# Another order of the parts in a convolution's list of four steps, with the table loads where they stand

## The chip, the cores and the metric

The kernel runs on one core of a Trainium2 chip. The time is device time of one execution, in microseconds (us); the median of three runs counts. Times in rows of the profile are from the start of the span.

## The reference: what is computed

A block with two halves. The first modulates a layer norm of the 2048 x 640 input by two rows computed from a condition, convolves each of the 640 channels along the 2048 positions with a kernel that a state-space model gives, adds a skip term and a gated residual. The second is a gated MLP on the same pattern. Cut to the first half:

```
h = layernorm(x) * (1 + ca) + sa
P = exp(dt * A * l)                       # 640 channels x 128 states x 2048 positions, complex
K = einsum("dn,dnl,dn->dl", C, P, dt * B).real
y = irfft(rfft(pad(h)) * rfft(pad(K)))[:2048] + h * Dskip
x = x + ga * y
h = layernorm(x) * (1 + cb) + sb
x = x + gb * ((silu(h @ w1) * (h @ w3)) @ w2)
```

## The kernel before, in words

A position is split as 64 a + b. So the convolution's kernel K for a channel is a product of a slow table (32 entries) and a fast one (64), each 128 states wide, and the states are summed by TensorE. The work goes by steps k of 16 channels, 40 in all. The transforms are matmuls with fixed tables, in two stages each way; their steps run ten behind (LAG), because the spectrum of a group of 128 channels needs the kernels of eight steps.

Each step has parts, and each part runs on one engine:

- PH (L442, POOL): the phases of the 16 channels, integer products and an add. Its buffer is one of four, freed by A2 of four steps earlier.
- AB, CO, SI (L450 to L461, ACT): absolute value of the phases, then cosine and sine. CO and SI use ACT's sine table; AB and plain copies run under any table.
- PA, PQ (L398, L409, PE): the exponents of the fast and the slow table, as small matmuls into PSUM; inside the list both write the one bank with the tag "B". XA, XQ (L421, L426, ACT): their exponentials, read from that bank into the table A. They use ACT's exponential table. So PA(k), XA(k), PQ(k), XQ(k), PA(k+1) follow one another by necessity.
- E1, E2, A1, A2 (L469 to L483, DVE): table times cosine (E1, E2, into E) and times sine (A1, A2, in place), in two pieces each.
- kg (L489, PE): the sum over states, 64 small matmuls. K (L499, DVE): out of PSUM, with skip term and gate. pt (L508, PE): the first transform stage of the kernel. uk (L516, ACT): copies it to where the spectra stand.
- st (L533, PE): the second stage, for input and kernel together, into one PSUM tile (L544). It loads its table from HBM (256 KB, three buffers), and every second st also loads a part of the next channel group's input spectra (u_load, L523).
- kc (L550, ACT): copies the kernel's spectrum out of PSUM. T, Y (L556, L565, DVE): products and sums of the complex product, partly in the same PSUM tile, which the next st reuses.
- iv (L574, PE): the first inverse stage; it loads its table (256 KB, three buffers). zt (L591, ACT): every second step, copies its result out of PSUM and stores it in two pieces to HBM.

A step's parts in the list carry a number: "XA+4" in round r is XA of step 4 r + 4. The list (L789) holds four steps' worth of words, and the loop at L797 runs it ten times. A word whose step is out of range, or was done before, does nothing; with what the code ahead of the loop has done, the rounds with r = 2 to 8 compute exponentials of steps 12 to 39, and r = 9 has none left. E1 of steps 24, 26, 28 and 30 also issues the load of one input tile (L802).

Inside the loop every instruction of PE, DVE, POOL and ACT is held in program order (`keep`, L113, and `act`, L117), so the list is the order on these four engines. DMAs go on SP's queue; the tile framework's planner places them by its own due times, and they wait there one behind the other. ACT's table loads are in no list: they are put in wherever an exponential follows a sine or cosine, or the other way round. Behind the loop (L805) the remaining convolution steps, loads for the MLP and the first row statistics run; the MLP follows.

Of the kernel before, what the change touches and what calls it, by code (L numbers as in the profile page):

```python
# [92 lines left out]
def tile_kernel(ctx: ExitStack, tc: tile.TileContext, a):  # L93
# [53 lines left out]
    uk = kp.tile([P, 3, NA, DC], F32, name="uk")  # L147
# [589 lines left out]
    for tk in range(LAG):  # L737
# [49 lines left out]


    ROUND = (  # L789
# [5 lines left out]
    ).split()  # L795
    in_order[0] = True
    for rnd in range(NS // EB):  # L797
# [293 lines left out]
```

## Time and profile before

| | us |
|---|---|
| median of 3 runs | 1058.37 |
| lowest, highest | 1058.28, 1059.08 |
| the profiled execution's own time | 1055.13 |
| its span, from the first to the last instruction | 1053.0 |
| mean granted TensorE clock | 0.921 |

Busy over the span: PE 963.9 us (92%), DVE 617.0 (59%), ACT 515.1 (49%), POOL 254.1 (24%). The rounds with exponentials and their table loads lie from about 169 to 380 us, the rest of the convolution to about 450, the MLP from about 467 to the end.

How to read it: in a windows row, the first number is the window's length, then each engine's busy time with its count of instructions, then the granted TensorE clock (1.00 is full), the DMA engines' busy share and GB/s. In a timeline row, start and duration, then engine, line, operation and tiles; in brackets the idle time before it and what ended it. In the chain of waits, each row is a piece of the chain that ended last, followed back from the end. In a waits row: who waited for whom, the total, how often, the longest. The tile `A` holds the tables, `cs` and `ph` cosine and sine, `pa` and `pq` the exponents, `pk` the sums over states, `p` the spectra, `pz` the inverse's first stage, `s` and `i` the loaded tables.

### The profile page before, as it was taken

The numbers are of one execution on the slowest core, as the hardware profiler recorded it, in microseconds if no ns is written. First come the engines' busy times: TensorE is split into PE (matmuls) and PEld (weight loads), VectorE is DVE, ScalarE is ACT, GpSimd is POOL, SyncE is SP. The second block draws the span as 40 slices with busy tenths as digits, with TensorE's granted clock in tenths as the row PEclk, the third lists the DMA queues.
The fourth block names the chain that finished last, engine by engine and source line by source line (L and its number), as shares of the span: only waits on it lengthen the run. The fifth ranks groups of instructions, "written<-read, shape, count | busy, mean of one in ns | idle before, by whom it ended". The sixth has DMA issues, their size and how long they took to land.

```text
span 1053.0 us, 20326 instructions
## 1 busy us (share of the span) xinstructions
PE 963.9 (92%) x8324; PEld 716.2 (68%) x8324; DVE 617.0 (59%) x1024; ACT 515.1 (49%) x697; POOL 254.1 (24%) x213
## 2 busy tenths in 40 slices
PE   5897888889888898759999999999999999999997
PEld 2444454666666675437778877788877788888886
DVE  4698774888788876655543465444555543533332
ACT  3658574898788873233234433234432344333331
POOL 1633431444343412131111111211111211111110
PEclk9655686999899989969999999999999999999999
DMA  9463493354354458877543364443353233433311
GB/s 268 161 251 115 179 249 91 113 161 130 111 144 134 129 159 187 267 188 212 144 123 97 89 205 132 119 119 88 101 186 100 83 96 98 139 99 101 95 43 50
DMA packets 107040, 146.29 MB, mean 139 GB/s; under 512 B 20836, under 2 KB 62948, under 8 KB 106948
## 3 DMA queue, kind: packets, MB, share of 16 engines
q1 hardware_dynamic: 104500, 140.09, 45.2%
q0 software_dynamic: 1024, 2.49, 0.9%
q10 hardware_dynamic: 1424, 2.43, 0.8%
q8 instruction: 65, 1.06, 0.4%
q14 instruction: 27, 0.22, 0.1%
HBM read 118.76 MB, written 26.21 MB: 138 GB/s over the span
## 4 chain that ended last, share of the span: by engine, by line
PE 74%; ACT 14%; DVE 6%; DMA 3%; issue 3%; POOL 0%; SPq 0%; DVEq 0%; ACTq 0%; POOLq 0%
PE acc L952 17%; PE pg L938 6%; PE pg L939 6%; PE pg L940 6%; PE pu L940 6%; PE pu L939 6%; PE pu L938 6%; PE p L544 5%; ACT cs L119 3%; PE pa L406 3%; ACT A L119 3%; ACT ph L119 2%; PE pq L418 2%; ACT L119 2%; PE pt L513 2%
## 5 line engine op out<-in xcount | busy, mean ns | idle before, releaser
L971 POOL TENSOR_TENSOR w<-w,gbr 128x512 f32<-128x512 f32 x55 | 83.7, 1522 | 395.6 <-DMA w<-in_w_dram 372.5
L446 POOL TENSOR_TENSOR ph<-thi,iota 128x1024 int32<-128x1024 int32 x40 | 85.4, 2134 | 207.0 <-DVE A L482 136.3
L938 PE MATMUL pg<-xh,gh 128*128 128x512 f32 x280 | 112.0, 400 | 0.1
L939 PE MATMUL pg<-xl,gh 128*128 128x512 f32 x280 | 109.6, 391 | 1.1 <-DVE xl L911 1.1
L923 ACT CAST gh<-wg 128x640 fp32r<-128x640 f32 x55 | 40.2, 731 | 141.8 <-PE pg L939 141.8
L940 PE MATMUL pg<-xh,gl 128*128 128x512 f32 x280 | 109.4, 391 | 0.0
L924 DVE TENSOR_TENSOR gl<-wg,gh 128x640 fp32r<-128x640 f32 x55 | 51.3, 933 | 89.5 <-ACT gh L923 88.4
L939 PE MATMUL pu<-xl,uh 128*128 128x512 f32 x260 | 101.2, 389 | 0.0
L938 PE MATMUL pu<-xh,uh 128*128 128x512 f32 x260 | 101.2, 389 | 0.0
L940 PE MATMUL pu<-xh,ul 128*128 128x512 f32 x260 | 101.1, 389 | 0.0
L924 DVE TENSOR_TENSOR wl<-w,wh 128x640 fp32r<-128x640 f32 x55 | 47.9, 870 | 88.6 <-ACT wh L923 88.6
L987 DVE TENSOR_TENSOR hf<-pu,sg 128x512 f32<-128x512 f32 x52 | 36.0, 692 | 102.8 <-PE pu L940 101.8
L544 PE MATMUL p<-uk,s 128*64 128x256 f32 x640 | 89.8, 430 | 1.6 <-DMA s<-in_s_dram 1.6
L923 ACT CAST uh<-wu 128x640 fp32r<-128x640 f32 x51 | 37.3, 732 | 106.4 <-issue 67.4
L952 PE MATMUL acc<-wh,hh 128*128 128x512 f32 x224 | 87.6, 391 | 0.0
L952 PE MATMUL acc<-wl,hh 128*128 128x512 f32 x224 | 87.2, 389 | 0.0
L923 ACT CAST wh<-w 128x640 fp32r<-128x640 f32 x55 | 40.1, 729 | 91.6 <-PE acc L952 91.1
L952 PE MATMUL acc<-wh,hl 128*128 128x512 f32 x208 | 80.9, 389 | 0.0
L544 PEld LDWEIGHTS p<-uk,s 128*64 128x64 f32 x640 | 47.7, 154 | 36.1 <-issue 15.7
L938 PEld LDWEIGHTS pg<-xh,gh 128*128 128x128 f32 x280 | 52.6, 188 | 17.8 <-issue 5.6
L585 PE MATMUL pz<-Y,i 64*128 64x128 f32 x640 | 48.0, 291 | 14.9 <-ACT zt L122 6.9
L939 PEld LDWEIGHTS pg<-xl,gh 128*128 128x128 f32 x280 | 52.6, 188 | 13.1 <-DVE xl L911 2.9
(203 smaller groups left out, 2072.8 us busy)
## 6 DMA issues: line engine op xcount, KB each, us to landing
wg<-in_wg_dram SPq DMA_DIRECT2D x55, 320.0 KB
wu<-in_wu_dram SPq DMA_DIRECT2D x51, 320.0 KB
w<-in_w_dram SPq DMA_DIRECT2D x51, 320.0 KB
us<-u SPq DMA_DIRECT2D x16, 640.0 KB
s<-in_s_dram SPq DMA_DIRECT2D x40, 256.0 KB
i<-in_i_dram SPq DMA_DIRECT2D x40, 256.0 KB
uk<-us SPq DMA_DIRECT2D x32, 256.0 KB
zs<-zt SPq DMA_DIRECT2D x32, 256.0 KB
```

The lines of the kernel that those rows point to most:

```text
L119: return tc.keep_in_program_order(S.activation(*args, **kw))
L446: hold(G.tensor_tensor(p, bc(thi[:, sl], 2, NPH), bc(iota, 1, SD), op=OP.mult))
L544: keep(PE.matmul(p2[par * 64:par * 64 + 64, pi, c, :], s2[:, pi * 2 + par, c * 64:c * 64 + 64], uk[:, 0:kn + 1:kn, f, :], start=True, stop ...
L585: ins = keep(PE.matmul(pz[:, par, (g % 2) * 2 + pi, :], i1[r, pi, c, :], Y[r, pi, c, :], start=(c == 0), stop=(c == 1), tile_position=(par ...
L923: S.copy(hi, src)
L924: V.tensor_tensor(lo, src, hi.bitcast(F32), op=OP.subtract)
L938: PE.matmul(ps, wh, xh, start=(i == 0), stop=False)
L939: PE.matmul(ps, wh, xl, start=False, stop=False)
L940: PE.matmul(ps, wl, xh, start=False, stop=(i == n - 1))
L952: PE.matmul(acc[k], lhs, rhs, start=(f == 0 and i == 0), stop=(f == NFT - 1 and i == len(terms) - 1))
L971: G.tensor_tensor(w2r[:, :512], w2r[:, :512], gbr, op=OP.mult)
L987: V.tensor_tensor(hf, pu, sg, op=OP.mult)
```

## The change

The one list is replaced by another; nothing else is touched. Both hold a word for every part of four steps. Some words carry another number, which moves them past the end of a round into the next: SI+3 in place of SI+7, iv+5 in place of iv+1.

```
     ROUND = (
-        "E1+2 iv+1 kc+2 CO+4 PH+5 T+2 pt+0 SI+4 PA+4 Y+2 kg+1 XA+4 E2+2 PQ+4 A1+2 XQ+4 uk+0 K+1 "
-        "PA+5 E1+3 st+3 XA+5 A1+3 zt+1 PQ+5 kc+3 A2+2 pt+1 XQ+5 T+3 PH+6 AB+5 PA+6 kg+2 Y+3 XA+6 "
-        "uk+1 K+2 PQ+6 E2+3 XQ+6 E1+4 AB+6 PA+7 A2+3 st+4 XA+7 E2+4 PH+7 PQ+7 kc+4 iv+2 XQ+7 T+4 "
-        "pt+2 A1+4 CO+5 kg+3 Y+4 uk+2 iv+3 E1+5 CO+6 st+5 SI+5 E2+5 K+3 AB+7 A2+4 pt+3 kc+5 PH+8 "
-        "zt+3 T+5 CO+7 iv+4 Y+5 uk+3 kg+4 SI+6 A1+5 st+6 AB+8 K+4 A2+5 SI+7 "
+        "E1+2 kc+2 pt+0 CO+4 PH+5 T+2 kg+1 SI+3 PA+4 K+1 SI+4 Y+2 uk+0 E2+2 st+3 E1+3 XA+4 A1+2 kc+3 "
+        "PQ+4 A2+2 pt+1 XQ+4 T+3 PH+6 PA+5 kg+2 XA+5 Y+3 uk+1 K+2 PQ+5 st+4 A1+3 XQ+5 zt+1 E1+4 AB+5 "
+        "PA+6 E2+3 pt+2 XA+6 A2+3 E2+4 kc+4 PQ+6 uk+2 PH+7 T+4 kg+3 XQ+6 AB+6 PA+7 K+3 iv+2 XA+7 AB+7 "
+        "Y+4 PQ+7 A1+4 st+5 XQ+7 A2+4 PH+8 kg+4 CO+5 iv+3 kc+5 K+4 CO+6 T+5 pt+3 zt+3 Y+5 uk+3 E1+5 "
+        "SI+5 st+6 CO+7 E2+5 A1+5 SI+6 iv+4 AB+8 A2+5 iv+5 "
     ).split()
```

## The prediction

> **What bounds the kernel now.** I read the page first, then the chain of waits inside the stretch that the list of four steps governs, then windows cut at the table loads, then windows cut along the clock's own changes.
>
> ```profile
> span 1053.0 us, 20326 instructions
> PEclk9655686999899989969999999999999999999999
> ```
>
> The clock row dips again and again before slice 15 and hardly after it, so the list's stretch has a clock matter of its own. In that stretch ACT changes its function table twice per round: to the exponential ahead of XA+4, to the sine ahead of CO+5. I call the time from the first to the second the exponential half, the rest the sine half. Seven rounds (steps 12 to 39) have an exponential half. Windows from load to load:
>
> ```profile
> core 0: us, PE busy (x) PEld busy (x) DVE busy (x) ACT busy (x) POOL busy (x), PEclk, DMA share, GB/s
> 169.00:188.63 19.63, 15.87 (x168) 10.35 (x170) 11.70 (x19) 11.79 (x15) 5.03 (x3) 0.74 0.36 107
> 202.74:219.55 16.81, 14.05 (x234) 9.19 (x234) 12.62 (x20) 12.63 (x16) 6.29 (x5) 0.90 0.33 94
> 233.66:250.46 16.80, 14.03 (x234) 9.30 (x234) 12.44 (x19) 12.63 (x17) 6.19 (x4) 0.90 0.35 96
> 264.57:284.21 19.64, 16.95 (x234) 11.26 (x234) 12.44 (x19) 12.69 (x16) 6.06 (x4) 0.74 0.35 100
> 298.32:315.12 16.80, 14.03 (x234) 9.18 (x234) 12.60 (x20) 12.63 (x17) 6.27 (x5) 0.90 0.47 134
> 329.23:346.02 16.79, 14.02 (x234) 9.29 (x234) 12.44 (x19) 12.63 (x17) 6.20 (x4) 0.90 0.34 95
> 360.12:379.76 19.64, 16.96 (x234) 11.26 (x234) 12.45 (x19) 12.69 (x16) 6.06 (x4) 0.74 0.29 80
> ```
>
> The seven add up to 126.11. A sine half is the gap between one row's end and the next row's start, 14.1 each, six of them. There are two kinds of exponential half: 16.8 at a granted clock of 0.90, and 19.64 at 0.74. Why the clock falls:
>
> ```profile
> 234.08:237.49 3.41, 1.42 (x58) 1.07 (x46) 3.38 (x5) 2.58 (x4) 0.60 (x1) 1.00 0.08 31
> 237.49:240.90 3.41, 3.41 (x16) 1.81 (x18) 2.37 (x3) 2.30 (x3) 0.79 (x1) 0.50 0.02 5
> 264.80:268.21 3.41, 1.56 (x68) 1.21 (x57) 3.38 (x6) 2.58 (x4) 0.79 (x1) 1.00 0.40 145
> 268.21:278.45 10.24, 10.10 (x92) 6.35 (x96) 4.71 (x7) 5.65 (x9) 2.95 (x2) 0.50 0.32 77
> 397.92:401.33 3.41, 1.93 (x66) 1.55 (x68) 3.34 (x6) 0.23 (x1) 0.00 (x0) 1.00 1.10 212
> ```
>
> The clock changes on a grid of 3.41 us. Where PE is busy for 1.42 or 1.56 of one such window, the next is granted half speed; where it is busy for 1.93, it is not. At half speed it stays for one window or for three. So the limit lies, in this trace, between 1.56 and 1.93 us of PE work per window, and every one of the seven exponential halves falls below it once. The chain of waits shows where and at what price:
>
> ```profile
> 233.66 1.28 ACT L119
> 234.95 1.03 ACT A L119
> ...
> 237.44 1.21 PE pa L406 x4
> 238.65 3.00 PE p L544 x16
> 241.65 0.66 PE pq L418 x7
> 242.31 1.02 PE pt L513 x16
> 243.34 0.68 PE pa L406 x4
> ...
> 247.27 1.90 PE p L544 x16
> ```
>
> Load, XA+4, PQ+4, XQ+4, PA+5: one bank holds both exponent sums, so PE waits for ACT's exponential each time, and the old list places nothing else in those waits. Then st+3 runs at half speed: 3.00 where the same sixteen matmuls take 1.90 at 247.27, and PA+5 takes 1.21 for 0.68. That is 1.63 per round; the 19.64 halves pay another 2.84. At full clock the old exponential half is 16.80 - 1.63 = 15.17.
>
> **The change part by part.** Nothing is added or removed; the words of one list stand in another order, so each engine runs the same instructions. On ACT, DVE, PE and POOL the list's order is the program's order, so I laid out each engine's words old and new, gave each the duration of its row, and followed what each waits for. Old list, same durations: the sine half comes to 14.09 against 14.11 measured.
>
> *The clock.* In the new list st+3 stands on PE between PA+4 and PQ+4, behind kg+1, so it runs under the table load and XA+4, where the old list has the bubble. What stands before it is Y+2, now behind K+1 on DVE:
>
> ```profile
> 244.12 0.41 DVE L569 TENSOR_TENSOR Y<-T,p 128x256 f32<-128x256 f32 x1
> 245.10 0.17 DVE L502 TENSOR_TENSOR pk<-pk,dz 128x4 f32<-128x4 f32 x1 [0.56 <-PE pk L495]
> 245.30 0.42 DVE L503 TENSOR_TENSOR K<-pk,gaT 128x256 f32<-128x256 f32 x1
> ```
>
> From kg+1's end K+1 takes 0.6 and Y+2, two such subtractions overlapping a little, another 0.75, PE has PA+4 (0.68) meanwhile, so it idles about 0.7; after st+3 it idles 0.6 to 0.8 until XA+4 is done. The worst 3.41 us window round that spot holds 2.0 to 2.1 us of PE work, above the 1.93 that kept full clock. Every other wait of the half has a piece of PE work in it: pt+1, kg+2, st+4, pt+2, kg+3, iv+2. I take no half-speed window: 7 x 1.63 + 3 x 2.84 = -19.9. Bounds: 0, if each stays, and a rise (below).
>
> *The exponential half at full clock.* PE's and ACT's chain in the new order, with these rows for kg and for the intervals on ACT:
>
> ```profile
> 220.94 0.32 PE L495 MATMUL pk<-E 128*32 128x64 f32 x8
> 221.97 1.16 PE L585 MATMUL pz<-Y,i 64*128 64x128 f32 x16
> ```
>
> ```profile
> 224.37 1.05 ACT L119 ACTIVATE cs<-ph 128x1024 f32<-128x1024 int32 x1
> 225.32 0.57 ACT L122 COPY kc<-p 128x512 f32<-128x512 f32 x1
> 238.69 1.02 ACT L119 ACTIVATE A<-pa 128x1024 f32<-128x1024 f32 x1 [0.82 <-PE pa L406]
> 239.61 1.01 ACT L122 COPY zt<-pz 128x1024 f32<-128x1024 f32 x1
> 249.84 0.60 ACT L119 ACTIVATE A<-pq 128x512 f32<-128x512 f32 x1
> ```
>
> Start to start, kg takes 1.03, XA 0.92, AB 0.95. The chain: load 1.29, XA+4 1.07 with its hand-over, PQ+4 0.66, pt+1 1.02, PA+5 0.70, XA+5 1.07, PQ+5 0.66, st+4 1.90, PA+6 0.70, XA+6 1.07, PQ+6 0.66, kg+3 1.03, PA+7 0.70, XA+7 0.92, AB+7 0.95, XQ+7 0.62: 15.0, and 15.1 with the 0.1 that a load loses by not overlapping. The moved pieces lie beside it: XQ+4 under pt+1, XQ+5, zt+1 and AB+5 under st+4 and PA+6, kc+4 and uk+2 under PQ+6 and kg+3, iv+2 under XA+7. So 15.17 becomes 15.1, 7 x 0.07 = -0.5, but with one more AB inside: three instead of two.
>
> *The sine half.* It loses that AB. ACT has no wait there in either list (its words lie end to end from the load on), so it shortens by 0.95, six times: -5.7.
>
> *uk+0 ahead of the load.* In the first round it delays the load by one 0.5 copy; later it only changes places. +0.5.
>
> *PH+7 ahead of AB+7.* PH+7 waits for A2+3, and POOL and DVE shut each other out:
>
> ```profile
> 248.21 2.22 POOL L446 TENSOR_TENSOR ph<-thi,iota 128x1024 int32<-128x1024 int32 x1 [5.07 <-DVE A L482]
> 250.50 1.05 POOL L447 TENSOR_TENSOR ph<-ph,phi 128x512 int32<-128x512 int32 x1
> 251.20 1.43 DVE L478 TENSOR_TENSOR A<-A,ph 128x1024 f32<-128x1024 f32 x1
> ```
>
> A1 takes 1.43 where POOL holds it to 251.55, else 1.2. In the new order A2+3 ends about 10.0 to 10.5 after the load, PH+7 takes 3.4 more, and AB+7 is due at 13.6: late by nothing to 0.5, behind it XQ+7 and the next load. I take the middle, 7 x 0.25 = +1.8.
>
> *The last round,* which has no exponents. kc+5 stands second after the sine load instead of sixth, so T+5 no longer waits there on DVE, E1+5 and E2+5 go behind it, and DVE is through its list about 2 earlier; PE's last steps follow DVE. -1.9, bounds 0 and -3.4 (that kc comes 3.4 sooner).
>
> *DMAs.* st brings its table load and, every second time, the spectra's loads; iv its table load; zt two stores; E1 four input loads late on. SP's order is the planner's, not the list's. In the old trace these loads follow the release of their buffer, three buffers ahead; the only load with little room in the new list is that of iv+5, released by iv+2 some 9.6 before it is used. I cost it at nothing; it is covered by those 9.6.
>
> Sum: -19.9 - 0.5 - 5.7 + 0.5 + 1.8 - 1.9 = -25.7. Against the profiled execution's own 1055.13 us that is 1029.4. The median of the runs shown, 1058.37, lies 3.24 above it, so 1032.7; I say 1032.5.
>
> **The rivals.**
> 1. *The low clock stays.* The new worst window is near the limit, and busy time may be the wrong measure, since these matmuls fill only part of the array; for it speaks that 10.10 busy of 10.24 still ran at half speed at 268.21; against it the 1.93 window. One half-speed window per round over pt+1, PA+5 and kg+2 costs about what it cost over PA+5 and st+3, 7 x 1.63 = 11.4: 1044. The Trainium skill bears on both sides: TensorE: Matmul & The Clock Gate (Why this matters for your kernels) holds that idle gaps over some 3 us cost the clock; here the window at 234.08 is idle for 3.41 - 1.42 = 1.99 us in all and the clock falls all the same, so the trace goes beyond that rule. The same page (A second HAM failure mode: psum-queue depth-cycling) says that small idles between matmul groups that cycle through PSUM banks are enough; the one shared bank stays, and by that rule this rival's time would come out.
> 2. *Slower: the low clock lasts.* If a dip comes each round at st+3 and recovery takes three windows each time, as in three of seven rounds now, each exponential half pays 1.63 + 2.84 = 4.47 on 15.1 plus 0.25: 19.8, 7 x 19.8 = 138.6 against 126.11. With the other terms (-5.7 + 0.5 - 1.9) it is +5.4: 1064. It decides from six of seven rounds with long dips on. Against it: four of seven recover after one window now.
> 3. *Late loads.* If the planner puts iv+5's load behind the stores of zt+3 and the spectra's loads, it comes late by one to two, and iv+5 delays pt+0, kg+1, K+1, Y+2 and st+3. The nearest row is of PE's waits from 165 to 455:
>
> ```profile
> PE pz L585 <- DMA i<-in_i_dram: 5.2, 2, 4.0
> ```
>
> Two waits, the longest 4.0. At 1.5 per round over seven: +10.5, 1043. Against it: the same view from 190 to 380 has no row of a load at all; these two lie behind it.
> 4. *The order does nothing.* If the chains that I followed are not those that bind, the time stays at 1058. Against it: the same walk gives the old halves within 0.05.
>
> **How the numbers follow.** Forecast 0.62; low clock stays, wholly or in some rounds, 0.18; late loads 0.10; slower 0.07; no effect 0.03. The forecast's own range is 1028 to 1037: PH+7 at nothing or 0.5, the last round at 0 or -3.4, one or two rounds with a dip. A measurement of this kernel tells some 0.2%, 2 us, from no change. For eight in ten I reach up over rivals 1 and 3, to 1046, and down to 1026, since the convolution's tail waits for loads (the 4.0 above) and may lose some of it. Faster 0.90, same 0.03, slower 0.07.
>
> **What would show it.** Exponential halves of 15.1 to 15.4 at a granted clock of 1.00; sine halves of 13.1 to 13.2; st+3 at 1.9 under the load and XA+4, with about 0.7 of PE idle on each side; AB+7 waiting for POOL by at most 0.5. Rows of 0.50 clock in steps 12 to 39 speak for rivals 1 or 2, PE waits for i or s loads for rival 3. I am wrong if the halves are right and the span is not, or if the halves stay at 16.8.

## The result and the profile after

| | before | after |
|---|---|---|
| median, us | 1058.32 (1054.56 to 1059.08, 4 runs) | 1029.32 (1026.20 to 1031.59, 4 runs) |
| the profiled execution's own time | 1055.13 | 1029.18 |
| its span | 1053.0 | 1027.4 |
| mean granted TensorE clock | 0.921 | 0.948 |

The ratio of after to before is 0.9731, 95% interval 0.9696 to 0.9765: faster. On the profiled executions it is 25.95 us less. Two lines of the page of after, the span and the clock row:

```profile
span 1027.4 us, 20301 instructions
...
PEclk9955688999999998789999999999999999999999
```

From slice 7 to slice 14 (counted from 0) the row is 9 throughout, where the row of before has an 8 in slices 10 and 14 (a dip of a few us shows little in a slice of 26); the dip that is left (slices 15 to 17) belongs to the tail behind the list. Windows of after, cut at its table loads (columns as in the prediction: length, busy times with counts, granted clock, DMA share, GB/s). The first seven rows are the exponential halves, the eighth is a sine half, the last is the whole stretch between two changes of the clock:

```profile
170.24:185.68 15.44, 14.71 (x260) 10.48 (x262) 14.08 (x23) 12.46 (x16) 6.23 (x4) 1.00 0.47 149
198.83:214.05 15.22, 14.11 (x258) 9.97 (x255) 13.12 (x22) 13.23 (x18) 6.23 (x4) 1.00 0.48 111
227.19:242.42 15.23, 14.19 (x258) 10.05 (x256) 13.21 (x22) 13.23 (x18) 6.22 (x4) 1.00 0.44 112
255.57:270.79 15.22, 14.18 (x258) 10.03 (x256) 13.19 (x22) 13.23 (x18) 6.23 (x4) 1.00 0.44 115
283.94:299.15 15.21, 14.18 (x258) 10.04 (x256) 13.19 (x22) 13.23 (x17) 6.23 (x4) 1.00 0.49 118
312.30:327.51 15.21, 14.17 (x258) 10.04 (x256) 13.18 (x22) 13.23 (x17) 6.22 (x4) 1.00 0.47 112
340.66:355.87 15.21, 14.18 (x258) 10.03 (x256) 13.19 (x22) 13.23 (x17) 6.23 (x4) 1.00 0.47 112
185.68:198.83 13.15, 11.32 (x244) 8.82 (x242) 11.27 (x20) 13.12 (x16) 6.76 (x4) 1.00 0.67 190
166.22:398.32 232.10, 205.71 (x3928) 150.95 (x3924) 193.94 (x321) 193.51 (x241) 91.73 (x64) 1.00 0.60 157
```

The seven add up to 106.74, 19.37 less than the 126.11 of before. Sine halves are 13.15 for 14.11. Full clock holds for 232.1 us without a break.

The place of the old bubble, one round, as PE's, DVE's, ACT's and POOL's timelines of after show it:

```profile
198.45 1.95 PE L544 MATMUL p<-uk,s 128*64 128x256 f32 x16 [0.80 <-PE pa L406]
201.20 0.39 PE L418 MATMUL pq<-r,lah 32*128 32x256 f32 x2 [0.80 <-ACT A L119]
```

```profile
197.94 0.41 DVE L569 TENSOR_TENSOR Y<-T,p 128x256 f32<-128x256 f32 x1
```

```profile
198.83 1.28 ACT L119 ACT_TABLE_LOAD   x1
200.12 1.02 ACT L119 ACTIVATE A<-pa 128x1024 f32<-128x1024 f32 x1
...
211.57 1.02 ACT L119 ACTIVATE A<-pa 128x1024 f32<-128x1024 f32 x1
212.50 1.05 ACT L119 ACTIVATE cs<-ph 128x1024 f32<-128x1024 int32 x1
```

```profile
211.38 1.05 POOL L447 TENSOR_TENSOR ph<-ph,phi 128x512 int32<-128x512 int32 x1
```

st+3 now takes 1.95 us, not 3.00, and lies under the load and XA+4, with 0.80 of idle PE on each side. The row puts the first of these waits down to PE's own PA+4, but what ended just ahead of st+3 is Y+2 on DVE, at 197.94 + 0.41 = 198.35, as the prediction has it. AB+7 (212.50) follows XA+7 without a gap, since POOL's part of PH+7 ended at 211.38 + 1.05 = 212.43.

Where some of the gain goes again is seen in the chain of waits behind the list. One row of before's chain, then one of after's, both of about the same moment of the convolution's tail:

```profile
417.08 11.76 DMA i<-in_i_dram
```

```profile
390.65 12.72 DMA zs<-zt
```

The list's last kc (step 41) starts 27.2 us earlier (381.31 for 408.48), the kc of step 43, the last ahead of these transfers, 26.2 earlier (389.92 for 416.13), but the MLP's first matmul only 24.3 earlier (442.55 for 466.82). Both chains go through a transfer here, and some 1.9 us of the gain are gone behind it.

### The profile page after: what moved, and what is told of

It is laid out like the page before. It is cut to its first block, busy times and chain, and to the rows that moved or that the text cites. A ratio compares the mean times of both kernels' runs of the same rounds, so it can differ in the third digit from the quotient of the medians.

```text
span 1027.4 us, 20301 instructions
## 1 busy us (share of the span) xinstructions
PE 945.2 (92%) x8324; PEld 707.8 (69%) x8324; DVE 607.3 (59%) x1024; ACT 512.7 (50%) x697; POOL 253.9 (25%) x213
## 4 chain that ended last, share of the span: by engine, by line
PE 72%; ACT 14%; DVE 6%; DMA 4%; issue 2%; POOL 1%; SPq 0%; DVEq 0%; ACTq 0%; POOLq 0%
PE acc L952 18%; PE pg L938 6%; PE pg L939 6%; PE pg L940 6%; PE pu L939 6%; PE pu L940 6%; PE pu L938 6%; ACT cs L119 3%; PE p L544 3%; ACT A L119 3%; ACT ph L119 3%; PE pa L406 2%; ACT L119 2%; PE pq L418 2%; DMA zs<-zt 2%
## 5 line engine op out<-in xcount | busy, mean ns | idle before, releaser
L544 PE MATMUL p<-uk,s 128*64 128x256 f32 x640 | 82.0, 400 | 16.5 <-PE pa L406 5.6
L940 PEld LDWEIGHTS pg<-xh,gl 128*128 128x128 f32 x280 | 52.5, 188 | 11.4
```

Of the source, the lines that this page charges most:

```text
L544: keep(PE.matmul(p2[par * 64:par * 64 + 64, pi, c, :], s2[:, pi * 2 + par, c * 64:c * 64 + 64], uk[:, 0:kn + 1:kn, f, :], start=True, stop ...
L940: PE.matmul(ps, wl, xh, start=False, stop=(i == n - 1))
```

## The experiments

The theory: the old list has one stretch per round with too little work on PE, the clock falls there, and the gain is the clock's. The rival: the order itself shortens the chain of dependences, and the clock only goes along. The medians of before beside these runs were 1056.30 to 1056.88; each ratio is against runs of before on the same chip.

**Three words of the old list moved.** st+3 goes behind kg+1, kc+3 behind XA+4, pt+1 behind PA+5; all else stands as before.

```
-... kg+1 XA+4 E2+2 PQ+4 A1+2 XQ+4 uk+0 K+1 PA+5 E1+3 st+3 XA+5 A1+3 zt+1 PQ+5 kc+3 A2+2 pt+1 XQ+5
+... kg+1 st+3 XA+4 kc+3 E2+2 PQ+4 A1+2 XQ+4 uk+0 K+1 PA+5 pt+1 E1+3 XA+5 A1+3 zt+1 PQ+5 A2+2 XQ+5
```

> The old list with three words moved: st+3 and kc+3 go under the table load and XA+4 (behind kg+1 and XA+4), pt+1 between PA+5 and PQ+5. Theory (the clock): no window of 3.41 us in the rounds holds less than 2.4 us of PE work, so the clock stays at 1.00 between the first exponential load and the last sine load; exponential halves 14.75 for 16.8 and 19.64, sine halves unchanged at 14.1. From the first load to the last transform that is 23.6 less than before: about 1035 us (1031 to 1036). Rival (the order as a whole, not this bubble): half-speed windows remain, one per round, at 1.63 each, so 11 later, 1046; or with long ones 1054.

Measured 1033.48 (1029.20 to 1034.91), ratio 0.9762 (0.9726 to 0.9798). Windows of this kernel, a sine half, an exponential half and the stretch of full clock:

```profile
185.35:199.46 14.11, 13.16 (x272) 10.07 (x272) 13.21 (x23) 14.08 (x17) 6.79 (x5) 1.00 0.66 188
199.46:214.21 14.75, 12.48 (x234) 8.56 (x234) 12.34 (x19) 12.42 (x17) 6.18 (x4) 1.00 0.45 110
167.85:406.77 238.92, 207.36 (x3942) 150.68 (x3938) 200.31 (x321) 194.41 (x242) 91.55 (x64) 1.00 0.59 159
```

Three words bring most of the whole change, with both halves as expected. They also move work into PE's waits, so this run alone does not yet part clock from order.

**One word of the old list moved.**

```
-... kg+1 XA+4 E2+2 PQ+4 A1+2 XQ+4 uk+0 K+1 PA+5 E1+3 st+3 XA+5
+... kg+1 st+3 XA+4 E2+2 PQ+4 A1+2 XQ+4 uk+0 K+1 PA+5 E1+3 XA+5
```

> The old list with one word moved: st+3 stands behind kg+1, nothing else. Followed at full clock the round is as long as the old one (29.31 against 29.25), so whatever this saves is clock alone. Its bubble moves behind PA+5, and the worst 3.41 us window holds 1.63 us of PE work, between the 1.56 that fell to half speed and the 1.93 that did not. Theory (the clock, set by work per window): either 1038 us with a clock of 1.00, or, if the limit is above 1.63, about 1058 with dips in rounds whose window lies so. Rival (order): 1058 at any clock.

Measured 1057.22 (1049.47 to 1064.95, 10 runs), ratio 1.0003 (0.9969 to 1.0037): no change. Theory with dips and rival both said 1058, so the time does not part them; the halves do. Windows of this kernel: two exponential halves, then windows of 3.41 us on the clock's grid and one low stretch:

```profile
200.27:215.51 15.24, 12.50 (x234) 8.58 (x234) 12.60 (x20) 12.32 (x17) 6.28 (x5) 1.00 0.44 107
229.61:250.11 20.50, 18.01 (x234) 12.13 (x234) 12.64 (x20) 12.51 (x16) 7.23 (x5) 0.67 0.32 84
...
204.68:208.09 3.41, 2.29 (x28) 1.57 (x28) 2.25 (x4) 3.06 (x5) 1.20 (x1) 1.00 1.03 216
334.39:337.80 3.41, 2.15 (x30) 1.53 (x28) 2.22 (x3) 3.12 (x5) 1.71 (x1) 1.00 1.05 230
337.80:341.21 3.41, 3.41 (x74) 2.59 (x76) 1.95 (x6) 2.24 (x3) 1.24 (x2) 0.50 0.59 154
235.40:249.06 13.66, 12.62 (x124) 8.40 (x126) 6.19 (x11) 7.62 (x11) 6.21 (x4) 0.50 0.34 87
```

The same words in the same order take 15.24 in one round and 20.50 in another of the same execution, at 1.00 and at 0.67 of the clock: five of the seven rounds dipped, for one window, for four (the last row) or for five. So order and clock do come apart. And the limit I had read off was wrong: the window from 334.39 holds 2.15 us of PE work, above my 1.93, and the next is at half speed; 2.29 at 204.68 was enough.

**st+3 taken back out of the bubble, in the new list.** kc+3 goes back with it, behind XQ+4.

```
-... uk+0 E2+2 st+3 E1+3 XA+4 A1+2 kc+3 PQ+4 A2+2 pt+1 XQ+4 T+3
+... uk+0 E2+2 E1+3 XA+4 A1+2 PQ+4 st+3 A2+2 pt+1 XQ+4 kc+3 T+3
```

> The new list with st+3 put back behind the exponential (behind PQ+4, kc+3 behind XQ+4). PE then stands still under the table load, 0.2 us of work in the worst window. Theory (the clock): exponential halves 17.0 at full clock plus 1.63 to 4.47 for the half-speed windows, 18.6 to 21.5, granted clock about 0.8 to 0.9; 1053 to 1073 us. Rival (the clock has another cause): only the 1.9 per round of uncovered matmuls returns, clock 1.00, 1042 us.

Measured 1059.04 (1054.68 to 1059.96, 10 runs), ratio 1.0016 (1.0002 to 1.003): the whole gain is gone. Windows of this kernel, two exponential halves, the window ahead of a dip and the dip:

```profile
169.34:188.07 18.73, 16.04 (x258) 11.01 (x260) 13.76 (x23) 12.54 (x16) 6.21 (x4) 0.91 0.43 129
201.22:221.18 19.96, 17.27 (x258) 12.07 (x260) 13.21 (x22) 13.34 (x18) 6.21 (x4) 0.83 0.36 86
199.66:203.07 3.41, 0.39 (x4) 0.00 (x0) 3.40 (x6) 3.38 (x5) 1.07 (x2) 1.00 0.06 21
203.07:209.90 6.83, 6.31 (x40) 4.40 (x40) 1.93 (x4) 1.65 (x3) 2.94 (x2) 0.50 0.01 3
```

Every round dips, four of them for one window, three for two. The seven halves add up to 134.6, 27.9 more than after's 106.74. Not all of that is the clock's: st+3's 1.9 us lie open again, and I had expected 17.0 per half at full clock, which would be 12.3 of the 27.9 and leave 15.6 for the dips. No run has this order at full clock, so this division is an estimate.

**One AB moved back into the sine half of the new list.** AB+7 goes from behind XA+7 to behind kc+5.

```
-... XA+7 AB+7 Y+4 PQ+7 ... iv+3 kc+5 K+4 ...
+... XA+7 Y+4 PQ+7 ... iv+3 kc+5 AB+7 K+4 ...
```

> The new list with AB+7 put back into the sine half (behind kc+5). Theory (ACT without a wait in the sine half, with waits in the exponential half): sine halves 14.1 for 13.15, exponential halves 15.1 to 15.2 as they are, clock 1.00; 5.7 later than the new list, 1035 us. Rival (AB costs the same in either place): 1029 us, the exponential halves 0.9 shorter.

Measured 1038.01 (1034.76 to 1043.55), ratio 0.9824 (0.978 to 0.9868). Six exponential halves are 15.19 or 15.20, sine halves 14.09 or 14.10: with AB+7 inside, the exponential half is no longer than without it, and the sine half gets its 0.95 back. The six sine halves together are 5.7 longer than after's, and the profiled execution is 5.99 above after's (1035.17 for 1029.18). The median lies 3 above the expected 1035; why the other executions were longer was not traced. The profiled one also dipped once in these rounds, and the exponential half behind that dip, at full clock, is 16.03. The windows ahead of the dip and in it, the like window two rounds earlier, and PE's timeline at the dip:

```profile
274.59:278.00 3.41, 1.60 (x24) 1.21 (x24) 3.27 (x6) 3.41 (x5) 0.86 (x1) 1.00 0.58 128
278.00:281.41 3.41, 3.41 (x20) 1.92 (x18) 3.12 (x4) 3.41 (x5) 0.94 (x1) 0.50 0.92 235
216.56:219.97 3.41, 1.60 (x22) 1.07 (x18) 3.01 (x6) 3.41 (x5) 0.32 (x1) 1.00 1.15 275
```

```profile
277.50 3.23 PE L544 MATMUL p<-uk,s 128*64 128x256 f32 x16 [1.81 <-ACT uk L122]
```

st+6 of a new channel group waits for uk+3, which stands behind the moved AB on ACT. Two rounds earlier it waits the same 1.81, the window holds the same 1.60, and the clock stays.

**Added work, no word moved.** In the old list the 64 matmuls of kg+1 are done twice in each of the seven rounds, in the idle time under the table load; then three times, the third pass behind PQ+4.

```
+        again = in_order[0] and s % EB == 1 and s + 3 < NS
+        for _ in range(2 if again else 1):
             (the 64 matmuls of kg into pk, start to stop)
```

For the third pass the function of PQ (L409) ends with the same 64 matmuls, in these rounds alone.

> The old list, word for word, but in the seven rounds with exponents the 64 small matmuls of kg+1 are done twice into the same bank (the second pass starts the sums anew, so the result is the same). It is added work: 1.03 us of PE per round, put where PE waits for the table load and XA+4 (1.30 of idle in the round at 233.66). Theory, the clock: the windows round the load, which hold 1.0 to 1.3 thousand columns of full-array work and 1.4 to 1.6 us of busy PE now, get 1.03 us and 1024 columns more and stay at 2016 or above (2.4 us busy); no half-speed window, exponential halves 15.2, sine halves 14.1, against before's 1056 about 19 to 20 less: 1036. Rival one, the order itself is what counts and the clock only goes along: more work under the same order gains nothing, 1056 or up to 7 x 1.03 = 7 more, 1063. Rival two, the limit lies above 2.4 us for work that fills as little of the array as kg does: the dips stay, 1056, exponential halves 16.8 and 19.6.

> As old_kg_twice, and a third pass of kg+1's 64 matmuls behind PQ+4, where PE waits 0.69 for XQ+4; 2.06 us of PE more per round than before, 0.3 to 0.4 of it in front of PA+5. In old_kg_twice the windows that began behind the second pass still lost the clock (2.31 us busy, full-array weight 1542 to 1836); with the third pass inside each of them they get about 1024 more. Theory, the clock: no half-speed window in the seven rounds, exponential halves 15.2 + 0.4 = 15.6, sine halves 14.1; against before 7 x 1.2 + 3 x 2.84, some 17 less: 1040, and 5 less than old_kg_twice although it does more work. Rival: what old_kg_twice won came from elsewhere, and the third pass costs its 0.4 or 1.03 per round: 1049 to 1053.

Twice: 1045.77 (1041.50 to 1049.39), ratio 0.9899 (0.9871 to 0.9928). Thrice: 1043.45 (1040.93 to 1046.76), ratio 0.989 (0.9846 to 0.9933). Windows of the kernel with two passes, two on the clock's grid and two exponential halves:

```profile
204.04:207.45 3.41, 2.31 (x114) 1.96 (x104) 3.38 (x5) 2.58 (x4) 0.65 (x1) 1.00 0.07 20
234.75:238.16 3.41, 2.31 (x22) 1.46 (x22) 3.27 (x5) 2.25 (x4) 0.00 (x0) 1.00 0.02 5
...
203.50:218.69 15.19, 13.31 (x298) 9.46 (x298) 12.60 (x20) 12.59 (x16) 6.29 (x5) 1.00 0.37 106
232.80:249.55 16.75, 14.87 (x298) 10.32 (x298) 12.44 (x19) 12.63 (x16) 6.20 (x4) 0.90 0.34 95
```

And of the kernel with three: the window ahead of the first round's dip, that dip, an exponential half, and the stretch of full clock.

```profile
169.51:172.92 3.41, 1.85 (x96) 1.56 (x88) 1.69 (x2) 2.58 (x4) 0.00 (x0) 1.00 0.85 307
172.92:179.74 6.82, 5.86 (x54) 2.90 (x42) 3.55 (x5) 1.55 (x3) 0.84 (x1) 0.50 0.03 8
202.67:218.12 15.45, 14.27 (x362) 10.40 (x362) 12.70 (x19) 12.64 (x16) 5.93 (x4) 1.00 0.39 108
179.74:415.26 235.52, 213.25 (x4594) 157.61 (x4592) 198.39 (x310) 189.17 (x234) 90.77 (x64) 1.00 0.57 155
```

The old list with more work to do is 11 and 13 us faster than without it, and not a word of it has moved. This settles the main question: what the old list lost in its exponential halves is the clock's. The sizes I had expected were too good. With two passes, windows that began behind the second pass still lost the clock (five dips in seven rounds, two halves of 15.19 and 15.45); with three, six of seven rounds stayed at full clock (four halves of 15.46, two of 15.92 and 16.44, whose extra I did not trace), and the first dipped: its first pass (168.05 to 169.1) and half of the second lay ahead of the window, and the third ran on past its end.

**uk+0 behind the load, and a longer search.** Two variants that try to beat the new list:

```
-... Y+2 uk+0 E2+2 st+3 E1+3 XA+4 A1+2 kc+3
+... Y+2 E2+2 st+3 E1+3 XA+4 uk+0 A1+2 kc+3
```

> The new list with one word moved: uk+0 from ahead of the table load to behind XA+4. Theory (the term of +0.5 of the prediction, whose first load came 1.24 later in place of 0.5): the load comes 0.5 earlier in the first round, the copy moves out of the sine half (13.15 to 12.7) into the exponential half (15.2 to 15.4), where part of it lies beside PE's work; from load to the last spectra's product 1.7 less than the new list, 1027.5. Rival: the copy stands on the chain of the exponential half in full, halves of 12.6 and 15.7, and only the first round's 0.5 is won: 1029.

The other variant is a list of its own; its opening, and the place by which it fell:

```
+"A1+2 SI+4 CO+4 kg+1 XA+4 pt+0 uk+0 T+2 Y+2 st+3 E2+2 kc+3 PH+5 K+1 PQ+4 E1+3 A2+2 pt+1 XQ+4 ...
+... A1+4 XA+6 A2+4 PQ+6 XQ+6 uk+2 PA+7 iv+2 XA+7 PQ+7 Y+4 PH+7 AB+7 kg+3 st+5 XQ+7 ..."
```

> Another order of the same parts, found by following the rows' durations as in the prediction: uk+0 behind the load, E2+3 and AB+5 and AB+6 placed so that PE's and ACT's words lie closer. Theory: exponential halves of 14.9, sine halves of 12.7, a period of 27.54 against 28.28, no window of 3.41 us with under 2.66 us of PE work, so no dip; 4.3 less than the new list over the stretch, 1025. Rival one: POOL and VectorE hold each other up more than the rows said, halves as in the new list, 1029. Rival two: loads of spectra come late under the shorter period, 1030 or more.

> The new kernel beside the others on one chip, for the comparison of the two variants: 1029, exponential halves 15.2, sine halves 13.15, granted clock 1.00 from the first table load to the last.

Measured beside each other: the new list 1030.23 (1029.90 to 1033.59), uk+0 behind 1030.83 (1025.69 to 1032.82), the searched list 1035.40 (1032.63 to 1036.03). With uk+0 behind, the halves came as expected, and from the first table load to the last it is 1.7 shorter than after, but the time is 3.3 above the 1027.5 that I had expected. The MLP's first matmul comes at 442.68, where after has 442.55: the tail gave the gain back. The last round also lost the clock once. An exponential half, a sine half, the window ahead of the dip and the dip:

```profile
199.36:214.65 15.29, 14.54 (x258) 10.38 (x260) 13.71 (x23) 13.70 (x19) 6.29 (x5) 1.00 0.48 114
214.65:227.32 12.67, 11.10 (x241) 8.35 (x236) 10.78 (x20) 12.64 (x14) 6.70 (x4) 1.00 0.68 199
368.89:372.30 3.41, 1.53 (x70) 1.18 (x64) 3.34 (x6) 1.41 (x2) 0.00 (x0) 1.00 0.91 187
372.31:375.72 3.41, 3.41 (x24) 2.29 (x22) 3.34 (x7) 0.59 (x1) 0.00 (x0) 0.50 0.62 199
```

The searched list kept full clock, but its exponential halves are 16.2 to 16.3 from the second round on. Its ACT, POOL and DVE timelines show by what:

```profile
215.53 1.06 ACT L119 ACTIVATE cs<-ph 128x1024 f32<-128x1024 int32 x1 [0.97 <-POOL ph L447]
```

```profile
213.59 1.91 POOL L447 TENSOR_TENSOR ph<-ph,phi 128x512 int32<-128x512 int32 x1
```

```profile
214.51 1.53 DVE L482 SCALAR_TENSOR_TENSOR A<-ph,A 128x512 f32<-128x512 f32 x1
```

AB+7 waits 0.97 for POOL, whose add takes 1.91 where it takes 1.05 when DVE leaves it alone; DVE's operation, 0.68 elsewhere, takes 1.53 beside it. They end at 215.50 and 216.04: the two hold each other up, as rival one had it, but it cost 1 us per half, and so more than rival one's 1029.

**The one dip, and pt done twice.** The uk+0 variant, with the 16 matmuls of pt for step 38 done twice. They were meant for the wait of the last round.

```
-        for g in range(4):
+        for _ in range(2 if s == NS - 2 else 1):
+            for g in range(4):
```

> new_uk0_behind, and the 16 matmuls of pt for step 38 done twice, in the 1.88 us in which PE waits for the DVE's last multiplication of the last round; there one half-speed window (372.31 to 375.72) cost the sixteen of st 3.23 for 1.95. Theory: that window stays at full clock, 1.3 less than new_uk0_behind's 1030.8, so 1029.5, a little under the new list's 1030.2, and no row of 0.50 before 395. Rival: the shorter rounds are given back in the tail, which waits for loads and stores, 1030.8.

Measured 1029.49 (1024.37 to 1031.33), ratio 0.9749 (0.9717 to 0.9781). The window in question, the stretch of full clock, and the doubled pt (32 matmuls) in PE's timeline:

```profile
369.05:372.46 3.41, 1.61 (x62) 1.31 (x64) 3.34 (x6) 1.21 (x2) 0.00 (x0) 1.00 0.98 208
167.66:396.35 228.69, 206.03 (x3941) 151.56 (x3938) 194.45 (x321) 193.48 (x241) 91.60 (x64) 1.00 0.60 159
```

```profile
373.60 1.97 PE L514 MATMUL pt<-s,K 128*64 128x128 f32 x32
```

The dip is gone and the time is the expected one, but not for the expected reason. The doubled pt runs behind st+4, from 373.60 on, and the wait of 1.88 (368.97 to 370.85) is as empty as before. The window that had been followed by a dip ends at 372.46, so the added work cannot have kept its clock. What differs is where the window falls: it holds 1.61 us of PE work against 1.53. This experiment shows nothing about filling a wait. Its interval overlaps that of the new list (0.9744 to 0.9786 in its second comparison): no version here beats the new list by more than can be measured.

## Why the prediction was right, and where not

The time said was 1032.5, measured 1029.32; the mechanism and its place were right. The sum of -25.7 against 25.6 between the two spans is closer than its terms deserve: two stretches that the sum left out, the tail (+1.9) and the MLP (-1.4), leave +0.6 between them, and the misses of the other terms add up to -0.5. That part is luck. Point by point, on the profiled executions:

- **The clock, the half at full clock, PH+7.** -19.9 - 0.5 + 1.8 = -18.6 was said for the seven exponential halves; they lost 19.37. No half-speed window came. The half is 15.21 to 15.23 from the second round on, where I had 15.1 and 0.25 for POOL. The term for PH+7 was wrong: AB+7 is late by nothing in the row at 212.50. POOL was through 0.07 ahead of it, so it holds by little, and the searched list shows it late by 0.97.
- **The sine half.** -5.7 said, -5.76 measured (6 x 0.96), and moving the AB back cost it again.
- **uk+0 ahead of the load.** +0.5 said; the first load came 1.24 later. But with uk+0 behind it, the first load came no earlier (170.77 and 170.80 for 170.24 and 169.73 with the new list). The first load's moment differs by such amounts from one execution to the next, and the half microsecond could not be told.
- **The last round.** -1.9 said; from the last table load to the list's last kc (step 41) 28.72 became 25.44, -3.3, near the bound of -3.4. Two steps further, at the kc of step 43, 2.3 of it are left (36.37 became 34.05).
- **DMAs at nothing.** Right in the rounds: PE's waits from 165 to 380 us have no row of a load, so rival 3 is out. Not right behind them: I gave the tail nothing in the sum, and from the kc of step 43 to the MLP's first matmul it took back 1.9. The MLP took 1.4 less (584.85 for 586.21); in the second profiled execution of the new list it took 586.06, so that is no part of the change. 1.24 (the first load) - 25.13 (the two kinds of halves) - 2.32 (to the kc of step 43) + 1.93 (the tail) - 1.36 (the MLP) = -25.6, the difference of the spans.
- **The offset of 3.24.** This is the step that failed. The sum against the profiled execution gave 1029.4, and that execution of after took 1029.18. Then came "The median of the runs shown, 1058.37, lies 3.24 above it, so 1032.7": I carried that distance over as though it were a property of the kernel. It was the distance of one draw from the middle of three others: in 19 runs before took 1050.06 to 1059.91, median 1056.46, only 1.3 above the profiled execution, and after's median is 0.14 above its own (its runs took 1026.20 to 1031.59). Dips that last one window or three, by chance, may be a part of before's spread; the rounds of 15.24 and 20.50 in one execution of the one-word variant fit that, but no trace shows what parted before's executions.
- **The limit of 1.56 to 1.93 us.** Wrong as a limit, though harmless here: the emptiest window round a table load of the new list, from 254.96, holds 2.38, more than the 2.0 to 2.1 that I had said. With one word moved, 2.15 was too little; of the five windows ahead of a dip there, four held more than my limit.
- **The rivals.** No effect, and late loads: excluded by the halves and the waits. Low clock stays, or lasts: not here, but moving st+3 back behind PQ+4 shows both at once, with dips in every round of one window or two, and 1059, no gain and no great loss; a part of that is st+3's own time, which lies open again.

The Trainium skill (TensorE: Matmul & The Clock Gate, A second HAM failure mode: psum-queue depth-cycling) tells of a kernel in which small idles between matmul groups that cycle through PSUM banks were enough to make the clock fall and rise again. Here such idles alone are not enough: the one shared bank stays in the new list, and so do waits of 0.80 on both sides of st+3, yet the clock holds for 232 us.

## What to carry to other kernels

Where the granted clock dips inside a loop, cut windows along the dips and look at what PE does just ahead of them: work that is due anyway, moved into that wait, can be worth more than its own length, and a list can be worth reordering for the clock alone. Leave a margin, since the windows' grid falls differently on each round and each execution. Do not carry the distance of one profiled execution from the median of a few runs over to the changed kernel.

## What the runs showed of the hardware

Busy time of PE in a window of 3.41 us does not decide by itself whether the next is granted full speed. The two windows with two passes of kg hold 2.31 us each; behind the one from 204.04 the clock stays, behind that from 234.75 it falls. With AB moved back, two windows of 1.60, each with a wait of 1.81 for uk, end differently as well (216.56 and 274.59). Nor does the longest idle stretch decide: it is 0.69 in the window from 234.75, which was followed by a dip, and 1.81 in that from 216.56, which was not.

I sorted the windows of the twelve traces by busy time (those on the clock's grid that lie wholly between 171 and 388 us and are at full speed: 704, of which 24 are followed by half speed). The best cut, near 1.6 us, leaves 9 on the wrong side: 8 dips that followed fuller windows, up to 2.31, and one window of 1.60 that kept the clock. A second measure weighs each matmul's columns by the share of the 128 x 128 array that it fills: 16 for one of kg (64 columns, 32 x 128), 128 for one of st (256 columns, 128 x 64). Its best cut leaves 4, 5 or 9, depending on whether a matmul across a window's edge is counted by its overlap, by its end or by its start. So it is not shown that the array's filling counts beside the time, and neither measure is the rule; a run that holds busy time and changes only the filling was not made. Some matmul records can be missing from traces, which blurs both measures.

Recovery differs too: at half speed PE is busy nearly throughout (3.41 of 3.41 at 337.80, 12.62 of 13.66 at 235.40), and it comes back after one window there and after four here. What decides that stays open.
